# Moving a raw-word load, a key split and one ranking step within a hand-ordered slot schedule

## The chip, the cores and the metric

The kernel runs on one core of one Trainium2 chip. TensorE (PE), VectorE (DVE), ScalarE (ACT) and GpSimd (POOL) each work through a queue of their own; SyncE (SP) issues all transfers between device memory and on-chip memory. The metric is the device time of one launch in microseconds (us), lower is better.

## What is computed

Three stages follow each other: clustered attention (a query sees only keys of its own cluster), a rational-function layer with two matrices, and a soft mixture of experts. The change lies in the first stage, which also turns the 64-bit weights of the second into 32-bit words on the side.

```python
def _attn_ref(q, k, v, centroids):          # q, k, v: (2, 8, 768, 64), centroids: (8, 16, 64)
    q_assign = np.argmax(np.einsum('bhsd,hcd->bhsc', q_n, c_n), axis=-1)
    k_assign = np.argmax(np.einsum('bhsd,hcd->bhsc', k_n, c_n), axis=-1)
    mask = q_assign[:, :, :, None] == k_assign[:, :, None, :]
    scores = np.where(mask, scale * np.matmul(q, k.transpose(0, 1, 3, 2)), -1e9)
    attn = softmax(scores)
    return np.matmul(attn, v)

def _moe_ref(x, w_in, w_out, a, b):         # w_in (512, 2048), w_out (2048, 512): float64 in memory
    h = x @ w_in
    g = (a[0] + a[1]*h + a[2]*h**2 + a[3]*h**3) / (1 + |b[0]|*|h| + |b[1]|*h**2 + 1e-6)
    return g @ w_out                        # then _moe2_ref: soft routing to 8 experts
```

## The kernel before

**Attention.** Two heads make a pair, and there are 8 pairs (0 to 7). The loop over `n` runs in slots, 12 for a pair, 96 in all; a slot treats one block of 128 queries of one head. In slot `n` PE transposes the exponentials of block `n` (`turn`, line 401, tile sT), multiplies queries by keys for block `n + 2` (`a1_mm`, lines 377 and 378, tile s) and adds to the product with v (`a2_av`, line 414). DVE takes the row maximum of s and copies it out (`a1_neg`, line 386, tile e), ACT takes the exponential (`a1_exp`, line 390) and copies the transposes to eT (`turned`, line 407). There is one bank pair for s and one for sT: PE may not begin the scores of block `n + 3` before DVE has read those of `n + 2`, nor the transposes of `n + 1` before ACT has copied those of `n`.

**Preparing a pair.** `prep(P)` prepares pair P while pair P - 1 (and the end of P - 2) is in the slots. It returns a table of rows (offset, engine, step), added at slot 12(P - 2) + 4. The steps are the ranking of clusters (`scores`, `scT`, `best`, and the three DVE steps `first(0..2)`, lines 268, 270 and 273, that make the one-hot rows), its transpose on PE (`ohT`, line 278), the copy and count on ACT (`count`, line 286, two halves), the mask weights on DVE (`masks`, lines 292 to 295, tile W), which wait for the count, and matmuls with W (`nonhot`, line 300; `alive`, line 313). `ksplit` splits the raw keys on POOL into a rounded part ka (line 239) and a rest kb (line 242), and SP sends them in six transfers (line 246) into the key operands, which pair P - 2 uses until its last scores. Pair 0 and pair 1 have orders of their own; pair 2 has the offsets of the early steps one higher (`b`).

**Decoding.** 32 blocks of raw 64-bit weight words, even ones of w_in and odd ones of w_out, go through `decode_steps`. Decode i has slot 2 + 53i // 20: three slots before it SP loads the raw words (`dma`, line 522, class "S"), in its slot DVE takes them apart (`bits`, lines 528 and 529), then `mant` (DVE, line 535) and `expo` (ACT, line 532) one slot later, `sign` (DVE, line 539) two, `value` (POOL, line 544) three, `parts` (POOL, lines 553 and 554) four. There are two raw buffers: the load for decode i waits until `sign` of decode i - 2 has read the buffer.

**What sets the order.** PE, ACT, DVE and POOL run in the order in which the loop writes the steps: in each slot first `run(n, (...))` with the classes D0, D, D1, D2 (DVE), G0, G (POOL) and S (raw loads), then the slot's main work with the classes A, P and T between. SP's order is set by the scheduler of the framework from the place in the program and its own estimate of when things are ready. A step of class G also issues the transfers that follow it (`ksplit`, `qsplit`, `parts`).

Of the kernel before, what the change touches and what calls it, by code (L numbers as in the profile page):

```python
# [58 lines left out]
def tile_kernel(ctx, tc, qT, kT, v, cenT, cenP, consts, constsb, ab, w_in, w_out, phi, w1, w2, out, dbg=None):  # L59
# [3 lines left out]
    B, NPB, _, S = qT.shape  # L63
    H = 2 * NPB
    D = v.shape[4]
# [70 lines left out]
    def load(p, names="kq"):  # L136
        b, hp = divmod(p, H // 2)
        r = raws.setdefault(p, {})
        for n in names:
            r[n] = raw_p.tile([128, S], F32, tag="raw" + n, name="raw" + n, bufs=2)  # L140
            SP.dma_start(r[n], (kT if n == "k" else qT)[b, hp])

    def load_v(p):
        b, hp = divmod(p, H // 2)
        vs[p] = v_p.tile([128, 2, 6, D], F32, tag="v", name="vt")
        SP.dma_start(vs[p], v[p])
# [68 lines left out]
    def prep(p):  # L215
# [6 lines left out]
        def tile_(pool, tag, shape, dt):  # L222
            hold[tag] = pool.tile(shape, dt, tag=tag, name=tag)
            return hold[tag]
# [28 lines left out]
        def best(c):  # L253
            if c == 0:
                tile_(s2_p, "mx", [128, 6, 4], F32)
                tile_(t_p, "eq", [128, 6, 4, 16], BF16)
            mv = hold.pop(("m", c))[:, 0:HS].rearrange("p (i g c) -> p i g c", i=3, g=4)[:, :, :, 0:16]
            mc = hold["mx"][:, 3 * c:3 * c + 3, :]
            DVE.tensor_reduce(mc, mv, AX.X, ALU.max)
            DVE.tensor_tensor(hold["eq"][:, 3 * c:3 * c + 3], mv,  # L260
                              mc.unsqueeze(3).to_broadcast([128, 3, 4, 16]), ALU.is_equal)

        def first(i):
            rank = cb[:, B_RANK:B_END].unsqueeze(1).to_broadcast([128, 24, 16])
            e3 = hold["eq"].rearrange("p i g c -> p (i g) c")
            m3 = hold["mr"] if i else tile_(s2_p, "mr", [128, 24], BF16)
            if i == 0:
                DVE.tensor_tensor(e3, e3, rank, ALU.mult)
            elif i == 1:
                DVE.tensor_reduce(m3, e3, AX.X, ALU.max)  # L270
            else:
                hold["oh"] = hold["eq"]
                DVE.tensor_tensor(e3, e3, m3.unsqueeze(2).to_broadcast([128, 24, 16]), ALU.is_equal)
# [60 lines left out]

        if p == 0:
            return first_pair(r, o, locals())
        b = 1 if p == 2 else 0
        return [
            (1 + b, "T", lambda: scores(0)),
            (2 + b, "A", lambda: scaled(0)),  # L340
# [3 lines left out]
            (4 + b, "D0", lambda: best(0)),  # L344
            (4 + b, "P", lambda: scT(1)),
            (5 + b, "D0", lambda: best(1)),
            (6, "D0", lambda: first(0)),
            (6, "G", ksplit),
            (7, "D0", lambda: first(1)),
            (8, "D0", lambda: first(2)),  # L350
            (8, "P", ohT),
            (9, "A", count),
            (10, "D0", masks),
            (10, "P", lambda: nonhot(0)),
            (11, "A", lambda: signed(0)),
# [12 lines left out]
    def a1_mm(u):  # L368
        p, idx = divmod(u, 12)
        half, rest = divmod(idx, 6)  # L370
        i, h = divmod(rest, 2)
        o = ops[p % NBUF][h]
        it = slice((3 * half + i) * 128, (3 * half + i + 1) * 128)
        ps = s1s[u] = psS[u == 1].tile([128, 2, 512], F32, tag="S", name="s1")
        for c in range(2):
            w = slice(c * HS, (c + 1) * HS)
            PE.matmul(ps[:, c, 0:HS], o["q1"][:, it], o["k1"][:, w], start=True, stop=False)  # L377
            PE.matmul(ps[:, c, 0:HS], o["q2"][0:80, it], o["k2"][0:80, w], start=False, stop=True)  # L378
# [9 lines left out]
    def a1_exp(u):  # L388
        g, rest = divmod(u, 6)
        ACT.activation(es[u], es[u], AF.Exp, scale=-1.0, bias=nvs[g][:, rest:rest + 1], accum_out=sums[g][:, rest:rest + 1])  # L390
# [3 lines left out]
    def turn(u):  # L394
        g, rest = divmod(u, 6)
        if rest == 0:
            eTs[g] = e_p.tile([128, 2, 6, HS], F32, tag="eT", name="eT", bufs=2)
        e = es.pop(u).rearrange("p c (j t) -> p (c j) t", j=3)
        ps = eTp[u] = psS[1].tile([128, 2, 512], F32, tag="S", name="sT")
        for j in range(6):  # L400
            PE.transpose(ps[:, j // 3, j % 3 * 128:(j % 3 + 1) * 128], e[:, j, :], ident)  # L401

    def turned(u):
        g, rest = divmod(u, 6)
        i, h = divmod(rest, 2)
        dst = eTs[g][:, h, :, i * 128:(i + 1) * 128].rearrange("p (c j) t -> p c j t", c=2)
        ACT.copy(dst, eTp.pop(u)[:, :, 0:HS].rearrange("p c (j t) -> p c j t", j=3))  # L407
# [37 lines left out]
    def a2_x(g):  # L445

        p, half = divmod(g, 2)
        b, c = divmod(p, H // 2)
        t0 = b * S + half * HS
        hold = {}  # L450

        def scale():
            hold["x"] = s2_p.tile([128, HS], F32, tag="x", name="x", bufs=1)
            DVE.tensor_tensor(hold["x"], av.pop(g)[:, 0:HS], Rs.pop(g), ALU.mult)

        def split():
            done = 0
            while done < HS:
                t, off = divmod(t0 + done, TB)
                n = min(HS - done, TB - off)  # L460
                src = hold["x"][:, done:done + n]
                dh, dl = xh[t][:, c, off:off + n], xl[t][:, c, off:off + n]
                POOL.tensor_scalar(dh, src, 1.0, 1.0, ALU.mult, ALU.mult)
                POOL.tensor_tensor(dl, src, dh.bitcast(F32), ALU.subtract)
                done += n

        return [(0, "D0", scale), (1, "G", split)]
# [11 lines left out]
    def idle(n):  # L479
        for _ in range(n):  # L480
            PE.matmul(rest_ps, zero[:, 0:128], zero, start=True, stop=True)
# [130 lines left out]
    def open_w():  # L612
        pctx.close()
        keep = ctx.enter_context(tc.tile_pool(name="keep", bufs=1, reuse_waits="tile"))
        return keep, bctx.enter_context(tc.tile_pool(name="wsp", bufs=2 * WAHEAD + 1, reuse_waits="tile"))

    def w_load(n):
        for a in range(2):
            wsp[n, a] = w_p.tile([128, NCC, 128], F32R, tag="w", name="w")
            SP.dma_start(wsp[n, a].rearrange("p c n -> p (c n)").bitcast(F32),  # L620
                         w_in2[n % NF][:, a].rearrange("p c n -> p (c n)"))
# [5 lines left out]
    def add(slot, steps):  # L627
        for off, eng, fn in steps:
            plan.setdefault(slot + off, {}).setdefault(eng, []).append(fn)

    def run(slot, engines):
        for eng in engines:
            for fn in plan.get(slot, {}).pop(eng, []):
                fn()
# [22 lines left out]
    for n in range(-LEAD, NSL + 6):  # L657
        p, k = divmod(n, 12)
        if n == -LEAD:
            load_v(0)  # L660
            load(2, "k")
        if n == 1:
            load(2, "q")
        if n == 2:
            load_v(1)
        if k == 4 and n > 0 and p + 2 < NP:
            add(n, prep(p + 2))
        if k == 6 and 0 < p < NP - 1:
            load_v(p + 1)
        if n > 0 and k == 0 and p + 2 < NP and p:  # L670
            load(p + 2, "q")
        if n > 0 and k == 1 and p + 2 < NP and p:
            load(p + 2, "k")
        if n == NSL - OPENW:
            keep, w_p = open_w()
            for i in range(WAHEAD):
                w_load(i)
        g, rest = divmod(n - 6, 6)
        if 0 < g < 2 * NP and rest == 0:
            add(n, a2_x(g - 1))  # L680
        if n == NSL + 4:
            add(n, a2_x(g))
        if n == NSL - 8:
            DVE.tensor_scalar(ncoef, coef, -1.0, None, ALU.mult)
            DVE.tensor_tensor(babs, coef[:, 4:6], ncoef[:, 4:6], ALU.max)
        run(n, ("D0", "D", "D1", "D2", "G0", "G", "S"))
        if 0 <= n < NSL:
            turn(n)
        if pend is not None:
            a1_exp(pend)  # L690
            pend = None
        if 0 <= n < NSL:
            turned(n)
        run(n, "A")
        if n + LEAD < NSL:
            pend = n + LEAD
            if n > 0 or n == -LEAD:
                a1_mm(pend)
            a1_neg(pend)
            if n < 0:  # L700

                a1_mm(n + 1 + LEAD)
        run(n, "P")
        if n >= NSL:
            if n < NSL + 2:
                a2_av(g, range(3 * rest, 3 * rest + 3))
        elif g >= 0:
            a2_av(g, (rest,))
        run(n, "T")
        if n < 6:  # L710
            idle(2 if n < -1 else 3)
# [448 lines left out]
```

## Time and profile before

| | us |
|---|---|
| median of three runs | 553.69 (551.89 to 554.3) |
| the profiled execution, its own time | 553.21 |
| span of its instructions | 551.2 |
| PE busy / DVE / ACT / POOL | 525.4 / 415.1 / 380.9 / 274.7 |

The span is the time from the first to the last instruction; 2.0 us of the execution lie outside it. The attention slots end near 298 us, the other two stages follow. A row of the timeline has its start, its length, the engine, the line, the operation and the tiles (written <- read), and in square brackets the idle time of the engine ahead of it and what ended that. PEld rows, the weight loads, are left aside: they overlap PE.

### The profile page before, as it was taken

What the parts mean: (1) busy time and instruction counts of PE and PEld (TensorE: products, weight loads), DVE (VectorE), ACT (ScalarE), POOL (GpSimd) and SP (SyncE); (2) the same over time, 40 slices, a digit from 0 to 9 for tenths busy, and PEclk for the clock granted to TensorE, in tenths of its full rate; (3) what the DMA queues carried; (4) which work ended last, traced back from release to release, by engine and by line L of the source; (5) the groups of instructions that cost most, each with busy time, mean ns of one, the idle gap of its engine ahead of it and who ended that gap; (6) DMA issues with size and microseconds to landing.
All of it is one profiled execution on the core that took longest, in us unless ns stands there. A gap on an engine that the chain in (4) does not pass through costs nothing.

```text
span 551.2 us, 10063 instructions
## 1 busy us (share of the span) xinstructions
PE 525.4 (95%) x3518; PEld 342.8 (62%) x3521; DVE 415.1 (75%) x801; ACT 380.9 (69%) x693; POOL 274.7 (50%) x314
## 2 busy tenths in 40 slices
PE   8989999899998999999999999999999999988994
PEld 3555566556565665665666777777777767643463
DVE  5688889789797788888742699999799988941143
ACT  2787887778878788797874688878587868820111
POOL 3436476567565576756623655565455535501000
PEclk9999999999999999999999999999999999998999
DMA  8949869588595885946431576766567656479996
GB/s 244 285 131 246 232 201 263 183 222 257 200 246 183 247 226 177 260 168 173 142 114 49 175 256 228 289 229 227 186 223 279 230 181 224 185 307 389 419 414 231
DMA packets 43282, 125.71 MB, mean 228 GB/s; under 512 B 6432, under 2 KB 7328, under 8 KB 38624
## 3 DMA queue, kind: packets, MB, share of 16 engines
q1 hardware_dynamic: 43232, 125.07, 69.7%
q8 instruction: 28, 0.46, 0.3%
q14 instruction: 22, 0.18, 0.1%
HBM read 89.66 MB, written 15.73 MB: 191 GB/s over the span
## 4 chain that ended last, share of the span: by engine, by line
PE 68%; DVE 11%; DMA 9%; ACT 6%; issue 2%; POOL 2%; SPq 1%; DVEq 0%; ACTq 0%; POOLq 0%
PE h L777 9%; PE h L780 8%; PE h L778 8%; PE av L414 7%; PE sT L401 7%; DMA raw<-w_out 4%; PE s L377 4%; PE gt L838 3%; PE s L378 3%; DVE e L386 3%; DMA raw<-w_in 3%; PE pb L1012 3%; PE pb L1083 3%; PE l L844 2%; PE dg L902 2%
## 5 line engine op out<-in xcount | busy, mean ns | idle before, releaser
L390 ACT ACTIVATE e<-e,nv 128x768 f32<-128x768 f32 x96 | 89.9, 936 | 45.2 <-DVE e L386 33.2
L386 DVE TENSOR_SCALAR_CACHE_REDUCE e<-s 128x768 f32<-128x768 f32 x96 | 91.5, 953 | 37.3 <-PE s L378 30.5
L401 PEld LDWEIGHTS sT<-cst,e 128*128 128x128 f32 x576 | 61.4, 140 | 51.3 <-ACT eT L407 19.1
L401 PE MATMUL sT<-cst,e 128*128 128x128 f32 x576 | 83.8, 282 | 0.7 <-ACT eT L407 0.6
L407 ACT COPY eT<-sT 128x768 f32<-128x768 f32 x96 | 75.7, 788 | 10.1 <-PE sT L401 9.2
L414 PE MATMUL av<-eT,vt 128*64 128x384 f32 x384 | 82.1, 510 | 0.0
L777 PE MATMUL h<-xh,w 128*128 128x512 f32 x192 | 80.6, 420 | 0.0
L377 PE MATMUL s<-k,q 128*128 128x384 f32 x192 | 73.3, 382 | 7.4 <-DVE pres L292 3.7
L544 POOL TENSOR_TENSOR w<-mh,ex 128x516 f32<-128x516 f32 x32 | 41.6, 1299 | 70.0 <-DVE ex L539 33.4
L778 PE MATMUL h<-xl,w 128*128 128x512 f32 x192 | 75.9, 395 | 0.0
L808 POOL TENSOR_SCALAR q<-u,babs 128x512 f32<-128x512 f32 x47 | 36.2, 770 | 73.9 <-ACT u L806 73.9
L378 PE MATMUL s<-k,q 80*128 80x384 f32 x192 | 64.8, 338 | 0.0
L810 POOL TENSOR_TENSOR q<-q,u 128x512 f32<-128x512 f32 x47 | 61.0, 1297 | 3.8
L780 PE MATMUL h<-xh,w 128*128 128x512 f32 x192 | 52.8, 396 | 0.0
L806 ACT ACTIVATE u<-h 128x512 f32<-128x512 f32 x47 | 27.9, 594 | 28.3 <-PE h L780 25.4
L777 PEld LDWEIGHTS h<-xh,w 128*128 128x128 f32 x192 | 36.2, 189 | 16.0 <-DVE r L826 3.4
L809 DVE TENSOR_TENSOR p<-p,h 128x512 f32<-128x512 f32 x47 | 32.1, 683 | 14.8 <-ACT p L807 14.6
L377 PEld LDWEIGHTS s<-k,q 128*128 128x128 f32 x192 | 36.4, 190 | 10.8 <-DVE e L386 4.8
L780 PEld LDWEIGHTS h<-xh,w 128*128 128x128 f32 x192 | 36.3, 189 | 8.9
L778 PEld LDWEIGHTS h<-xl,w 128*128 128x128 f32 x192 | 36.2, 189 | 7.2 <-issue 0.5
L817 ACT ACTIVATE r<-q,epsc 128x512 f32<-128x512 f32 (+1 forms) x49 | 33.8, 690 | 8.1 <-POOL q L810 6.7
L825 DVE SCALAR_TENSOR_TENSOR p<-p,ncoef,r 128x512 f32<-128x512 f32 (+1 forms) x49 | 35.8, 731 | 2.4 <-ACT r L818 1.8
(179 smaller groups left out, 1003.0 us busy)
## 6 DMA issues: line engine op xcount, KB each, us to landing
wt<-w SPq DMA_DIRECT2D x32, 1024.0 KB, 7.6
w<-w_in SPq DMA_DIRECT2D x96, 256.0 KB, 3.1
raw<-w_in SPq DMA_DIRECT2D x16, 512.0 KB, 5.0
raw<-w_out SPq DMA_DIRECT2D x16, 512.0 KB, 5.4
w_in<-w SPq DMA_DIRECT2D x16, 512.0 KB, 4.0
k<-ka SPq DMA_DIRECT2D x32, 192.0 KB, 5.9
q<-qh SPq DMA_DIRECT2D x28, 192.0 KB, 5.2
w_out<-w SPq DMA_DIRECT2D x16, 256.0 KB, 4.6
```

The costliest lines, as they stand in the source:

```text
L377: PE.matmul(ps[:, c, 0:HS], o["q1"][:, it], o["k1"][:, w], start=True, stop=False)
L378: PE.matmul(ps[:, c, 0:HS], o["q2"][0:80, it], o["k2"][0:80, w], start=False, stop=True)
L386: DVE.tensor_scalar(e, s1s.pop(u)[:, :, 0:HS], -1.0, None, ALU.mult, ALU.min, accum_out=nvs[g][:, rest:rest + 1])
L390: ACT.activation(es[u], es[u], AF.Exp, scale=-1.0, bias=nvs[g][:, rest:rest + 1], accum_out=sums[g][:, rest:rest + 1])
L401: PE.transpose(ps[:, j // 3, j % 3 * 128:(j % 3 + 1) * 128], e[:, j, :], ident)
L407: ACT.copy(dst, eTp.pop(u)[:, :, 0:HS].rearrange("p c (j t) -> p c j t", j=3))
L414: PE.matmul(av[g][64 * h:64 * h + 64, 0:HS], vs[g // 2][:, h, j, :], eTs[g][:, h, j, :], start=(j == 0), stop=(j == 5))
L544: POOL.tensor_tensor(w.rearrange("p (r n) -> p r n", r=3), hold["mh"].bitcast(F32), hold["ex"].bitcast(F32), ALU.mult)
L777: PE.matmul(h, wh[:, c, :], xh[t][:, c, :], start=(c == 0), stop=False)
L778: PE.matmul(h, wh[:, c, :], xl[t][:, c, :], start=False, stop=False)
L780: PE.matmul(h, wl[:, c, :], xh[t][:, c, :], start=False, stop=(c == NCC - 1))
L810: POOL.tensor_tensor(q, q, u, ALU.mult)
```

## The change

Three edits. The raw load of a slot (class S) is written ahead of the slot's POOL steps (class G), so ahead of the transfers which those steps issue. `ksplit` moves from offset 6 to 8: slot 12(P - 2) + 12 where it was 12(P - 2) + 10, for pairs 2 to 7. For pairs 3 to 7 the steps `first(0)`, `first(1)`, `first(2)`, `ohT` and `count` move one slot forward (earlier); `masks` and all after it stay. Pairs 0 and 1 keep their order; nothing is added or removed.

```diff
-        b = 1 if p == 2 else 0
+        b, c = (1, 0) if p == 2 else (0, -1)
...
-            (6, "D0", lambda: first(0)),
-            (6, "G", ksplit),
+            (6 + c, "D0", lambda: first(0)),
+            (8, "G", ksplit),
...
-            (9, "A", count),
+            (9 + c, "A", count),
...
-        run(n, ("D0", "D", "D1", "D2", "G0", "G", "S"))
+        run(n, ("D0", "D", "D1", "D2", "G0", "S", "G"))
```

SP's queue where pair 3's keys are sent (slots 20 to 25): raw_148 is the buffer of even decodes, raw_149 that of odd ones, `w_in<-w` sends a decoded block away, `k<-ka` and `k<-kb` are the key operands. Before:

```order
L522 DMA raw_148<-w_in 128x1024
L555 DMA w_in_146<-w_1111 128x1024
L246 DMA k_1_0_127<-ka 64x768 x2
L246 DMA k_1_1_131<-ka 64x768 x2
L246 DMA k_1_0_128<-kb 64x768
L246 DMA k_1_1_132<-kb 64x768
L522 DMA raw_149<-w_out 128x1024
L548 DMA w_out_147<-w 128x512
```

The same place after the change:

```order
L522 DMA raw_148<-w_in 128x1024
L555 DMA w_in_146<-w_1113 128x1024
L522 DMA raw_149<-w_out 128x1024
L548 DMA w_out_147<-w 128x512
L246 DMA k_1_0_127<-ka 64x768 x2
L246 DMA k_1_1_131<-ka 64x768 x2
L246 DMA k_1_0_128<-kb 64x768
L246 DMA k_1_1_132<-kb 64x768
```

The load of decode 9 (raw_149) and the sending of decode 7 stand ahead of the six key transfers instead of behind them.

SP's queue at pair 5 (slots 44 to 50), where the loads are those of decodes 17, 18 and 19. Before:

```order
L522 DMA raw_149<-w_out 128x1024
L548 DMA w_out_147<-w 128x512
L246 DMA k_1_0_127<-ka 64x768 x2
L246 DMA k_1_1_131<-ka 64x768 x2
L246 DMA k_1_0_128<-kb 64x768
L246 DMA k_1_1_132<-kb 64x768
L522 DMA raw_148<-w_in 128x1024
L141 DMA rawk<-kT 128x768
L555 DMA w_in_146<-w_2089 128x1024
L522 DMA raw_149<-w_out 128x1024
```

After:

```order
L522 DMA raw_149<-w_out 128x1024
L548 DMA w_out_147<-w 128x512
L522 DMA raw_148<-w_in 128x1024
L555 DMA w_in_146<-w_2082 128x1024
L246 DMA k_1_0_127<-ka 64x768 x2
L246 DMA k_1_1_131<-ka 64x768 x2
L246 DMA k_1_0_128<-kb 64x768
L246 DMA k_1_1_132<-kb 64x768
L522 DMA raw_149<-w_out 128x1024
L141 DMA rawk<-kT 128x768
```

The load of decode 18 comes ahead of the keys; that of decode 19 (the second raw_149) now stands right behind them.

ACT's queue around pair 3's count (slots 24 and 25): e is the exponential, eT the copy of transposes, wT a copy for the decoding, oT with cnt the count. Before:

```order
L390 ACTIVATE e,ssum<-e,nv 128x768
L407 COPY eT<-sT 128x6x128
L573 COPY wT<-mf 128x512
L286 ACTIVATE oT,cnt<-mb 64x3x128 x2
L390 ACTIVATE e,ssum<-e,nv 128x768
```

The same five rows after the change:

```order
L286 ACTIVATE oT,cnt<-mb 64x3x128 x2
L390 ACTIVATE e,ssum<-e,nv 128x768
L407 COPY eT<-sT 128x6x128
L573 COPY wT<-mf 128x512
L390 ACTIVATE e,ssum<-e,nv 128x768
```

The count moved ahead of one exponential and one copy of the main work; the other engines' queues move in the same way.

## Rows read from the trace of the kernel before

**Rows 1.** Window: length, then busy us of PE, PEld, DVE, ACT, POOL; clock; DMA:

```profile
57.15:298.00 240.85, 232.08 (x1566) 148.14 (x1565) 190.92 (x395) 192.17 (x353) 142.37 (x168) 1.00 0.68 198
```

**Rows 2.** Timeline: PE's waits at the preparation of pairs 3 to 7:

```profile
100.01 0.45 PE L377 MATMUL s<-k,q 128*128 128x384 f32 x1 [2.22 <-DVE pres L292]
...
123.82 0.44 PE L377 MATMUL s<-k,q 128*128 128x384 f32 x1 [0.25 <-DVE e L386]
...
135.71 0.34 PE L300 MATMUL mf<-oT,W 80*128 80x384 bf16 x1 [0.35 <-DVE W L295]
...
171.02 0.45 PE L377 MATMUL s<-k,q 128*128 128x384 f32 x1 [1.49 <-DVE pres L292]
...
206.79 0.34 PE L300 MATMUL mf<-oT,W 80*128 80x384 bf16 x1 [0.46 <-DVE W L295]
...
209.46 0.44 PE L377 MATMUL s<-k,q 128*128 128x384 f32 x1 [0.73 <-DVE e L386]
...
242.17 0.34 PE L300 MATMUL mf<-oT,W 80*128 80x384 bf16 x1 [0.37 <-DVE W L295]
```

**Rows 3.** Timeline: DVE's two long waits for raw words (decodes 9 and 18):

```profile
97.79 0.69 DVE L528 TENSOR_SCALAR ex<-raw 128x516 int32<-128x516 int32 x1 [2.00 <-DMA raw<-w_out]
...
168.81 0.69 DVE L528 TENSOR_SCALAR ex<-raw 128x516 int32<-128x516 int32 x1 [1.34 <-DMA raw<-w_in]
```

**Rows 4.** Timeline: DVE's waits for the count, pairs 4, 6 and 7:

```profile
135.00 0.20 DVE L293 TENSOR_SCALAR pres<-cnt 32x1 f32<-32x1 f32 x1 [1.30 <-ACT oT L286]
...
206.08 0.20 DVE L293 TENSOR_SCALAR pres<-cnt 32x1 f32<-32x1 f32 x1 [1.49 <-ACT oT L286]
...
241.20 0.20 DVE L293 TENSOR_SCALAR pres<-cnt 32x1 f32<-32x1 f32 x1 [0.70 <-ACT oT L286]
```

**Rows 5.** Timeline: SP issuing keys and raw loads, pairs 3 and 5:

```profile
88.20 1.31 SPq L246 DMA_DIRECT2D k<-kb  x2
90.05 0.33 SPq L522 DMA_DIRECT2D raw<-w_out  x1
...
161.34 0.48 SPq L522 DMA_DIRECT2D raw<-w_in  x1
```

**Rows 6.** Timeline: DVE's sign steps that free the buffers of decodes 9 and 18:

```profile
86.84 1.30 DVE L539 SCALAR_TENSOR_TENSOR ex<-raw,ex 128x516 int32<-128x516 int32 x1
...
158.46 0.68 DVE L539 SCALAR_TENSOR_TENSOR ex<-raw,ex 128x516 int32<-128x516 int32 x1
```

**Rows 7.** Transfers: KB and us to landing of the loads issued at 199.58 and 207.36:

```profile
raw<-w_out SPq DMA_DIRECT2D x1, 512.0 KB, 5.7
...
raw<-w_in SPq DMA_DIRECT2D x1, 512.0 KB, 3.1
```

**Rows 8.** Timeline and group of line 286: ACT and PE around pair 3's count:

```profile
95.69 0.78 ACT L407 COPY eT<-sT 128x768 f32<-128x768 f32 x1
...
96.92 0.88 PE L401 MATMUL sT<-cst,e 128*128 128x128 f32 x6
...
L286 ACT ACTIVATE oT<-mb 64x384 bf16<-64x384 bf16 x16 | 7.7, 482 | 3.7 <-PE mb L278 3.6
```

**Rows 9.** Timeline of POOL and DVE around pair 5's split:

```profile
154.92 0.83 POOL L239 TENSOR_SCALAR ka<-rawk 128x768 fp32r<-128x768 f32 x1
155.83 2.42 POOL L242 TENSOR_TENSOR kb<-rawk,ka 128x384 fp32r<-128x384 f32 x2
...
155.99 1.40 DVE L535 SCALAR_TENSOR_TENSOR mh<-raw,mh 128x516 f32<-128x516 uint32 x1
...
164.85 1.60 POOL L554 TENSOR_TENSOR w<-w,w 128x512 fp32r<-128x512 f32 x1
...
175.46 0.69 DVE L528 TENSOR_SCALAR ex<-raw 128x516 int32<-128x516 int32 x1
...
177.50 0.96 DVE L386 TENSOR_SCALAR_CACHE_REDUCE e<-s 128x768 f32<-128x768 f32 x1 [0.75 <-PE s L378]
```

**Rows 10.** Group of line 268: the step first(0):

```profile
L268 DVE TENSOR_TENSOR eq<-eq,cb 128x384 bf16<-128x384 bf16 x8 | 3.4, 427 | 0.1
```

More of the change, by code (lines that the diff above doesn't have):

```diff
@@ L346, in prep @@
             (5 + b, "D0", lambda: best(1)),
-            (6, "D0", lambda: first(0)),
-            (6, "G", ksplit),
-            (7, "D0", lambda: first(1)),
-            (8, "D0", lambda: first(2)),
-            (8, "P", ohT),
-            (9, "A", count),
+            (6 + c, "D0", lambda: first(0)),
+            (8, "G", ksplit),
+            (7 + c, "D0", lambda: first(1)),
+            (8 + c, "D0", lambda: first(2)),
+            (8 + c, "P", ohT),
+            (9 + c, "A", count),
             (10, "D0", masks),
```

## The prediction

> **What bounds the kernel now.** I read first the busy time of the engines over the attention slots: in 240.9 us from slot 12 on PE is busy 232.1, DVE 190.9, ACT 192.2, POOL 142.4, at a granted clock of 1.00 [rows 1]. PE bounds this stage, and an edit that takes nothing out of PE's work can win no more than the 8.8 us for which PE stands idle there. The change lies in this stage alone; the two later stages run after it and would shift as a whole.
>
> Second, where PE waits in the slots that the change touches, those around the preparation of pairs 3 to 7 [rows 2]. The reader is to see two long waits, 2.22 us (pair 3) and 1.49 us (pair 5), at a scores matmul, and short ones: 0.35, 0.46 and 0.37 us at the first matmul with the mask weights W (pairs 4, 6, 7), and 0.73 us at a scores matmul right after pair 6's. The 0.25 us at 123.82 is another kind, DVE late with a row maximum.
>
> Third, what DVE waits for just before each. The label of the two long ones, `pres`, is the next row on DVE and no cause. Ahead of it DVE had stood 2.00 and 1.34 us for raw words [rows 3], and everything behind, the row maximum that frees the scores bank included, was late by that much. Ahead of the short ones DVE stood 1.30, 1.49 and 0.70 us for ACT's count [rows 4]. So two causes: two raw loads that land late, and a count that ends late.
>
> Fourth, why the loads are late. The load for decode 9 was issued at 90.05, right behind the last key transfers at 88.20 [rows 5], while `sign`, which frees its buffer, ended at 86.84 + 1.30 = 88.14 [rows 6]. It landed 97.79 - 90.05 = 7.7 us later. For decode 18 `sign` ended at 158.46 + 0.68 = 159.14 [rows 6], the issue came at 161.34 [rows 5], the landing 7.5 us later at 168.81 [rows 3]. A load with nothing ahead of it lands in 3.1 us [rows 7]. So 1.9 and 2.2 us were lost in SP's queue, and some 4 us more behind the bytes of six key transfers.
>
> **The change, part by part.**
>
> *Loads ahead of the keys.* At pair 3 the load of decode 9, at pair 5 that of decode 18 now stands ahead of the six key transfers, and the keys are split two slots later. It can go at 88.1 and 159.1 and has 97.79 - 2.00 - 88.1 = 7.7 us and 168.81 - 1.34 - 159.1 = 8.4 us until DVE asks. Even 5.7 us, the landing of a load issued behind keys but with little else ahead [rows 7], fits. I take both DVE waits as gone. For PE that is 2.22 + 1.49 = 3.7 us, unless something else is late next.
>
> *What is late next there: ACT.* The count now stands ahead of an exponential and a copy eT of the main work. It is two halves of 0.48 us, 1.0 us together [rows 8]. At pair 3 the copy ended at 95.69 + 0.78 = 96.5 and PE began the next transposes, which need its bank, at 96.92. Delayed by 1.0 the copy ends near 97.5: PE waits 0.6 us where it did not. I charge 0.6 at pair 3 and, as an estimate by the same row, 0.6 at pair 5; zero if ACT runs earlier because DVE does. At pairs 4, 6 and 7 I charge nothing: DVE, for whose row maxima ACT's exponentials wait, stands idle 0.70 to 1.49 us there [rows 4] and will run earlier by that. Without this cover it would be 0.6 each.
>
> *The count one slot forward.* A slot is 240.9 / 84 = 2.9 us [rows 1], so the count ends 1.0 to 2.9 us earlier, against DVE waits of 0.70 to 1.49. All three should go, and with them PE's 0.35 + 0.46 + 0.37 and, since DVE is then on time, the 0.73 behind pair 6's: 1.9 us in all.
>
> *The ranking one slot forward.* DVE's work is the same, but the slot that has `best(1)` now also has `first(0)`, 0.43 us [rows 10], ahead of its row maximum. At pair 4 that row maximum is the one for which PE already waits 0.25 at 123.82, so this wait should grow by 0.4. At pairs 3, 5, 6 and 7 PE shows no wait there; I charge 0.4 for one of the four, and keep 0 and 1.6 as the bounds.
>
> *The key split two slots later.* Its operands are used from ten slots later on, some 29 us: nobody waits for the keys themselves. What waits is what is queued behind: on POOL the steps xh, rb and `value`, which come 0.8 + 2.4 = 3.3 us later [rows 9] and are asked for more than a slot afterwards; on SP the loads behind the keys. At pair 5 that is decode 19. POOL ends `parts` at 164.85 + 1.60 = 166.4, then ka and kb at 169.7, two kb transfers of 0.65 each follow [rows 5], and the load goes near 171.0. With 3.1 us it lands at 174.1, with 5.7 at 176.7; DVE asks for it at 175.46 - 1.34 = 174.1 [rows 9]. So DVE waits 0 to 2.6 us, of which 0.75, its present wait for PE at 177.50, is covered [rows 9]: 0 to 1.9 us on PE. I take 0, since the slots behind it hold extra PE work, and keep 1.9 for the range and for a rival.
>
> [...] At 155.99 the DVE step of line 535 took 1.40 us beside POOL's kb; the sign step of the same shape took 0.68 alone at 158.46 [rows 6, 9]. Kb will now meet another DVE step, so I count 0.7 lost for 0.7 won. [...]
>
> **The sum.** Won: 3.7 + 1.9 = 5.6. Given back: 0.6 + 0.6 on ACT, 0.4 + 0.4 on DVE, 2.0. Net 3.6 us. The span goes from 551.2 to 547.6, the execution, with 2.0 us around the span, from 553.2 to 549.6. The profiled execution is 0.5 below the median of 553.69, so the median goes to **550.1 us**. With nothing given back it is 548.1; with four times 0.4 on DVE and 0.6 at four pairs on ACT (1.6 + 2.4 = 4.0, net 1.6) 552.1.
>
> **The rivals.**
>
> 1. *The wait moves from decode 18 to decode 19.* For it: SP's new order at pair 5, and a POOL that is 3.3 us later. Against it: DVE has slack two slots on. Price 1.9 us: 550.1 + 1.9 = 552.0.
> 2. *Kb meets the wrong DVE steps.* In the slots right behind the split DVE makes W and the row maxima for which PE waits; if at each of the six pairs the 0.7 us falls on PE's path, while in the place before it lay beside PE work, the price is 6 x 0.7 = 4.2: 554.3, no change. Against it: the split met such a step before as well [rows 9], so the place changes and not the number.
> 3. *The loads land as late as before.* If the landing is set by the bytes already under way (the query transfers ahead) and not by SP's order, only the count's 1.9 is won and the 2.0 lost: 553.8. Against it: the key bytes were among those ahead.
> 4. *Slower: loads caught behind later keys.* The keys now go in the slots in which the next loads are due (decodes 10, 15 and 19 at pairs 3, 4 and 5). A load that needs the 7.7 us seen at decode 9 instead of 3.1 loses 4.6 us; if its time before DVE asks is shorter than that by 2.5 at three pairs, 7.5 us are lost against 3.6 won: 557.6. It decides where POOL ends kb later than the `sign` that frees the next buffer. At pair 5 it does by the working above; elsewhere I find it only by a little or not at all.
>
> **How the numbers follow.** Forecast 0.52 (548.1 to 552.1); rival 1 0.15; rival 2 0.12; rival 3 0.12; rival 4 0.09. A measurement of this kernel can tell 0.5%, 2.8 us, from no change: faster is below 550.9, slower above 556.5. Of the forecast's own range some 0.42 of its 0.52 lies below 550.9, of the rivals 0.04: 0.46 faster. Slower is most of rival 4: 0.08. The rest, 0.46, is the same. The range is 547.5 to 554.5: below it I leave 0.03, above it rival 4 and the upper tail of rivals 2 and 3, 0.15.
>
> **What would show it.** In the profile after: DVE's idle ahead of line 528 without a 2 us entry, decode 9's load issued near 88, decode 18's near 159 on the old clock; PE's waits at `pres` gone; DVE's wait at line 293 gone for pairs 3 to 7 and still there for pairs 1 and 2. New waits of PE at sT for a copy eT, 0.6 each, would show ACT's price; a DVE wait for raw words near slot 52 rival 1; line 535 and 539 with a higher mean rival 2. I am wrong if PE's idle time in the attention stage does not fall by 2 to 6 us, or if it falls and the later stages give it back.

## The result and the profile after

The changed kernel took 547.78 us (median of four runs, 546.47 to 549.21) against 553.85 for the kernel before on the same chip: a ratio of 0.9897, 95% interval 0.9852 to 0.9943, faster by 1.0% or 6.1 us. Repeated later it gave 548.11 us and 0.9895 (0.9860 to 0.9929). The prediction said 550.1 us, 547.5 to 554.5.

The profiled execution took 547.26 us, its span 545.5. The window table of both kernels, from the first PE transposes of slot 12 to those of slot 95 (length, then busy us of PE, PEld, DVE, ACT, POOL; granted clock; DMA), first before, then after:

```profile
57.15:294.93 237.78, 229.01 (x1550) 146.06 (x1548) 190.26 (x393) 190.99 (x351) 142.29 (x167) 1.00 0.69 201
```

```profile
56.72:290.71 233.99, 228.77 (x1551) 145.85 (x1549) 189.86 (x393) 190.89 (x351) 144.92 (x170) 1.00 0.69 204
```

PE's busy time differs by 0.2 us; the time in which it stands idle fell from 8.8 to 5.2 us, so these slots are 3.8 us shorter. Of the 5.95 us between the two profiled executions, 3.79 lie here, 0.43 ahead of slot 12 (near 52 us PE waits 0.82 us for query operands before and 0.33 after), 1.48 behind slot 95, 0.25 outside the span.

PE's waits that answer to [rows 2], timeline after:

```profile
64.23 0.34 PE L300 MATMUL mf<-oT,W 80*128 80x384 bf16 x1 [0.45 <-DVE W L295]
...
96.18 0.87 PE L401 MATMUL sT<-cst,e 128*128 128x128 f32 x6 [0.26 <-ACT eT L407]
98.36 0.34 PE L300 MATMUL mf<-oT,W 80*128 80x384 bf16 x1 [0.61 <-DVE W L295]
121.75 0.44 PE L377 MATMUL s<-k,q 128*128 128x384 f32 x1 [0.66 <-DVE e L386]
...
191.26 0.44 PE L377 MATMUL s<-k,q 128*128 128x384 f32 x1 [0.22 <-DVE e L386]
204.71 0.44 PE L377 MATMUL s<-k,q 128*128 128x384 f32 x1 [0.17 <-DVE e L386]
228.64 0.45 PE L377 MATMUL s<-k,q 128*128 128x384 f32 x1 [0.20 <-DVE e L386]
231.89 0.44 PE L377 MATMUL s<-k,q 128*128 128x384 f32 x1 [0.35 <-DVE e L386]
```

The 2.22 and 1.49 us at `pres` are gone, so are the waits for W at pairs 4, 6 and 7 and the 0.73 behind pair 6's; pair 2's W wait (64.23) was there before. From pair 3 on the waits sum to 2.47 us, against 5.87 in [rows 2]. Waits of PE that both kernels have are left out, as in [rows 2] (line 313 near 140 and 175, line 377 near 252).

SP and DVE where the loads of decodes 9, 18 and 19 are issued, answering to [rows 5, 6], the transfers issued at 86.97 and 156.57 (KB, us to landing), and the two kinds of DVE wait that are left, answering to [rows 3, 4]:

```profile
86.25 0.69 DVE L539 SCALAR_TENSOR_TENSOR ex<-raw,ex 128x516 int32<-128x516 int32 x1
86.97 0.33 SPq L522 DMA_DIRECT2D raw<-w_out  x1
...
155.85 0.70 DVE L539 SCALAR_TENSOR_TENSOR ex<-raw,ex 128x516 int32<-128x516 int32 x1
156.57 0.33 SPq L522 DMA_DIRECT2D raw<-w_in  x1
...
165.91 1.33 SPq L246 DMA_DIRECT2D k<-kb  x2
167.33 0.54 SPq L522 DMA_DIRECT2D raw<-w_out  x1
```

```profile
raw<-w_out SPq DMA_DIRECT2D x1, 512.0 KB, 4.2
...
raw<-w_in SPq DMA_DIRECT2D x1, 512.0 KB, 3.4
```

```profile
63.53 0.20 DVE L293 TENSOR_SCALAR pres<-cnt 32x1 f32<-32x1 f32 x1 [1.49 <-ACT oT L286]
...
173.74 0.69 DVE L528 TENSOR_SCALAR ex<-raw 128x516 int32<-128x516 int32 x1 [1.91 <-DMA raw<-w_out]
```

Both loads now go within 0.03 us of the `sign` that frees their buffers, land 4.2 and 3.4 us later (7.7 and 7.4 before), and DVE does not wait for them. The count wait is left at pairs 0, 1 and 2 alone. One raw wait is new: decode 19's load stands behind the moved keys and lands 6.3 us after its issue, so DVE stands 1.91 us. PE shows no wait for it.

### The profile page after: what moved, and what is told of

The parts are those of the page before. It is cut to its first block, busy times and chain, and to the rows that moved or that the text cites. A ratio compares the mean times of both kernels' runs of the same rounds, so it can differ in the third digit from the quotient of the medians.

```text
span 545.5 us, 10069 instructions
## 1 busy us (share of the span) xinstructions
PE 524.1 (96%) x3518; PEld 342.3 (63%) x3521; DVE 414.0 (76%) x801; ACT 381.0 (70%) x693; POOL 274.5 (50%) x314
## 4 chain that ended last, share of the span: by engine, by line
PE 75%; DVE 11%; ACT 5%; DMA 4%; issue 3%; SPq 1%; POOL 1%; DVEq 0%; POOLq 0%; ACTq 0%
PE av L414 10%; PE sT L401 9%; PE h L777 9%; PE h L780 8%; PE h L778 8%; PE s L377 5%; PE s L378 4%; DVE e L386 4%; PE gt L838 4%; PE pb L1083 3%; PE pb L1012 3%; PE l L844 2%; PE dg L902 2%; PE mf L230 1%; ACT e L390 1%
```

## The experiments

Slots are cut at the start of PE's transposes (line 401) in the one execution that was profiled of each kernel; slots 20 to 95 are called the stage below. The changed kernel has two such profiles, and their slots 20 to 95 differ by 1.0 us (210.35 and 211.32), so a difference of that size in this column is not shown by it alone. The ratio is to runs of the kernel before on the same chip; "all its runs" are the 88 made beside the experiments, on four chips. The last column counts runs whose mean granted clock was 0.994 or less.

| kernel | time, us | ratio to before (95%) | slots 20 to 95, us | low-clock runs |
|---|---|---|---|---|
| before (all its runs) | 553.82 | | 213.8 | 52 of 88 |
| loads first alone | 551.59 | 0.9962 (0.9931 to 0.9993) | 213.1 | 1 of 10 |
| keys later alone | 552.90 | 0.9968 (0.9942 to 0.9994) | 215.4 | 0 of 10 |
| ranking earlier alone | 550.91 | 0.9970 (0.9934 to 1.0005) | 213.1 | 4 of 10 |
| loads and keys | 553.74 | 1.0004 (0.9976 to 1.0031) | 214.8 | 2 of 10 |
| keys and ranking | 548.55 | 0.9893 (0.9843 to 0.9943) | 210.4 | 1 of 4 |
| all three, again | 548.11 | 0.9895 (0.9860 to 0.9929) | 211.3 | 0 of 6 |
| before, waits filled | 551.87 | 0.9987 (0.9957 to 1.0018) | 213.0 | 1 of 12 |
| pair 5's keys later still | 549.20 | 0.9925 (0.9896 to 0.9955) | 212.0 | 2 of 10 |
| ranking in shared slots | 548.29 | 0.9909 (0.9873 to 0.9945) | 210.4 | 2 of 6 |
| the same, last pair as before | 545.44 | 0.9856 (0.9817 to 0.9894) | 209.6 | 0 of 5 |
| after, long waits put back | 556.88 | 1.0059 (1.0030 to 1.0089) | 219.0 | 12 of 12 |
| after, long waits elsewhere | 556.38 | 1.0055 (1.0027 to 1.0083) | 218.9 | 8 of 12 |

**Loads first, alone.**

```diff
-        run(n, ("D0", "D", "D1", "D2", "G0", "G", "S"))
+        run(n, ("D0", "D", "D1", "D2", "G0", "S", "G"))
```

> Only the raw load is written ahead of the slot's POOL steps; the key split and the ranking stay. In SP's queue this moves decode 9's load ahead of two of the six key transfers at pair 3, decode 18's ahead of one at pair 5. Theory K (the waits for raw words come from the key transfers ahead, so the split's two slots take them away, and this edit does little): DVE's wait at decode 9 falls from 2.00 to about 0.5 and at decode 18 from 1.34 to about 0.7, PE's last transposes start 1 to 2 us before 294.9. Theory L (the place of the load in the slot takes them away): both waits 0, last transposes near 291.5, 3.5 us earlier. The count's waits stay at 1.3 to 1.5 in both.

PE's two waits at `pres` and DVE's raw wait for decode 9, timeline:

```profile
95.33 0.69 DVE L528 TENSOR_SCALAR ex<-raw 128x516 int32<-128x516 int32 x1 [0.81 <-DMA raw<-w_out]
97.55 0.45 PE L377 MATMUL s<-k,q 128*128 128x384 f32 x1 [0.75 <-DVE pres L292]
...
169.86 0.44 PE L377 MATMUL s<-k,q 128*128 128x384 f32 x1 [0.99 <-DVE pres L292]
```

The edit shortens the waits and does not remove them: SP now sends load 9 ahead of two of the six key transfers, no more, and load 18 ahead of one, and they land 7.8 and 8.1 us after their issue, as late as before. Slots 20 to 32 are 1.4 us shorter, but slots 32 to 44 are 1.0 longer. There `first(2)` (line 273), 0.56 us in the kernel before, began while POOL's `value` (line 544) was under way:

```profile
126.16 1.29 POOL L544 TENSOR_TENSOR w<-mh,ex 128x516 f32<-128x516 f32 x1 [1.52 <-DMA w_out<-w]
126.32 1.55 DVE L273 TENSOR_TENSOR eq<-eq,mr 128x384 bf16<-128x384 bf16 x1
```

In the kernel before `value` began at 128.42, 0.03 us behind `first(2)` at 128.39, and it was `value` that took longer (1.69 us for 1.29). In all the stage is 0.8 us shorter.

**Keys later, alone.**

```diff
-            (6, "G", ksplit),
+            (8, "G", ksplit),
```

> Only the key split moves two slots later. Theory K: both waits for raw words are gone (0.2 at most), a new one of some 1.9 us comes for decode 19, the count's waits stay and new ones appear at pairs 3 and 5, where DVE is now early; PE's last transposes start 2.5 to 3.5 us before 294.9. Theory L: the waits stay at 2.0 and 1.3, last transposes within 0.5 of 294.9.

The raw waits of decodes 9 and 18 are gone, so it is this edit that clears SP's queue; yet slots 20 to 95 became 1.6 us longer, where a gain was expected. The median of its runs is 0.8 us below the kernel before all the same, since none of them had a low clock; its runs at 0.997 or more have a median of 552.7 us, against 551.4 for those of the kernel before on that chip, so they are 1.3 us longer too. The cause stands on DVE, shown here at pairs 4 and 5, in the rows around `first(2)` with POOL's `value` and `parts` (lines 544 and 554), and DVE's count wait and PE's wait for W behind it:

```profile
126.35 1.29 POOL L544 TENSOR_TENSOR w<-mh,ex 128x516 f32<-128x516 f32 x1 [2.84 <-PE mf L569]
126.69 1.37 DVE L273 TENSOR_TENSOR eq<-eq,mr 128x384 bf16<-128x384 bf16 x1
...
134.12 0.20 DVE L293 TENSOR_SCALAR pres<-cnt 32x1 f32<-32x1 f32 x1 [1.49 <-ACT oT L286]
135.02 0.34 PE L300 MATMUL mf<-oT,W 80*128 80x384 bf16 x1 [0.74 <-ACT e L390]
...
162.54 1.28 POOL L554 TENSOR_TENSOR w<-w,w 128x512 fp32r<-128x512 f32 x1
162.59 1.65 DVE L273 TENSOR_TENSOR eq<-eq,mr 128x384 bf16<-128x384 bf16 x1
```

With the split gone from its old place, POOL's two-input steps run just when DVE comes to `first(2)`, which takes 1.37 and 1.65 us there; at pair 6 it meets `value` (1.06 us), at pair 7 the second half of the split itself (1.40 us). It ends 0.42 us after POOL's step in both places shown (128.06 against 127.64, 164.24 against 163.82). The transpose of the one-hot rows and the count are later by that. At pair 3 it is W itself (line 295) that meets `parts`: 1.41 us, 0.46 in the kernel before. PE pays at W: 0.86, 0.74 (its row names ACT's e), 0.37, 0.46 and 0.66 us at pairs 3 to 7, where [rows 2] has 0, 0.35, 0, 0.46 and 0.37, and besides 0.35 to 0.40 at three row maxima that had no wait. One new wait cost more than its bracket: slot 37 grew by 0.64 us for 0.35; the scores matmul had begun 0.24 us before the end of the transposes ahead of it. The transfers gained what this edit promised; DVE lost more.

**Ranking earlier, alone.**

```diff
-        b = 1 if p == 2 else 0
+        b, c = (1, 0) if p == 2 else (0, -1)
...
-            (6, "D0", lambda: first(0)),
+            (6 + c, "D0", lambda: first(0)),
```

`first(1)`, `first(2)`, `ohT` and `count` get the same `+ c`.

> Only the ranking steps and the count come one slot earlier for pairs 3 to 7. Additive theory: the count's waits of DVE (1.30, 1.49, 0.70) are gone, both waits for raw words stay near 2.0 and 1.3, and PE's last transposes start 0.7 to 1.5 us before 294.9 (1.9 won, 0.4 to 1.2 given back on DVE and ACT). Rival (the two causes hide each other): no gain, because the raw waits grow by what the count no longer costs: within 0.3 of 294.9.

All count waits of pairs 3 to 7 are gone. Of the raw waits, decode 9's stays:

```profile
97.57 0.69 DVE L528 TENSOR_SCALAR ex<-raw 128x516 int32<-128x516 int32 x1 [1.82 <-DMA raw<-w_out]
...
97.88 0.87 PE L401 MATMUL sT<-cst,e 128*128 128x128 f32 x6 [0.72 <-ACT eT L407]
99.78 0.44 PE L377 MATMUL s<-k,q 128*128 128x384 f32 x1 [1.04 <-DVE pres L292]
```

The stage is 0.8 us shorter, the same as with the first edit. Here too `first(2)` meets `value`, at pairs 3 and 5 (0.98 and 1.12 us).

**Loads and keys, without the ranking**, to see whether the parts add.

```diff
-            (6, "G", ksplit),
+            (8, "G", ksplit),
...
-        run(n, ("D0", "D", "D1", "D2", "G0", "G", "S"))
+        run(n, ("D0", "D", "D1", "D2", "G0", "S", "G"))
```

> The first two edits (raw load ahead, key split later) without the ranking edit. Theory M (the edits need each other: once the raw words are in time, DVE stands for the count instead, and the keys' POOL steps slow DVE in the slots that first(2) still fills): no raw wait of 0.5 us or more in pairs 3 to 5, count waits of 1.2 to 1.5 at pairs 4, 6 and 7, and the stretch from slot 20 to slot 95 takes 214.5 to 216, as with the key split alone (215.4), against 210.4 in the whole change. Additive theory: 211 to 212.

No gain in time, 1.0 us more in the stage, with count waits of 1.48, 1.48 and 1.24 us at pairs 4, 6 and 7: nearly the second edit's picture, with `first(2)` at 1.05 to 1.39 us at pairs 4 to 7.

**Keys and ranking, without the loads** (against the changed kernel).

```diff
-        run(n, ("D0", "D", "D1", "D2", "G0", "S", "G"))
+        run(n, ("D0", "D", "D1", "D2", "G0", "G", "S"))
```

> The change without its first edit: key split later and ranking earlier, the raw load written behind the POOL steps as before. Theory K: the same as the whole change, last transposes within 0.3 of 290.7, ratio to the kernel before near 0.99. Theory L: the waits for raw words are back, 294 or so.

This is the whole change: the stage's 210.4 us are those of the changed kernel, the time differs by less than the interval. With the keys out of the way, SP's order differs from that of the changed kernel in one row only. So the second and third edits make the gain together (−3.4 us in the stage, against +1.6 and −0.8 alone). The runs at a clock of 0.997 or more on that chip, few as they are, say the same: medians of 551.4 us before, 552.7 with the second edit, 550.1 with the third, 548.4 with both. The reason that the rows show is that the third takes `first(2)` away from the POOL steps that the second brings to it: over pairs 3 to 7 `first(2)` takes 2.8 us in the kernel before, 4.2 with the first edit alone, 6.0 with the second, 3.8 with the third and 3.4 with the second and third together. The first adds nothing that can be measured.

**Pair 5's keys two slots later still** (on the changed kernel), to remove the new wait of 1.91 us.

```diff
-            (8, "G", ksplit),
+            (10 if p == 5 else 8, "G", ksplit),
```

> The whole change, with the key split of pair 5 alone another two slots later, so that decode 19's load stands ahead of its transfers. If DVE's wait of 1.91 us for decode 19 is covered by its slack to PE: that wait is gone and the stretch from slot 44 to slot 56 stays at 34.6 (within 0.2). Rival (it cost PE time): the stretch falls by 0.5 to 1.9 us.

Decode 19's wait is gone, and slots 44 to 56 rose from 34.64 to 35.38 us, with two PE waits that the changed kernel lacks:

```profile
168.09 0.44 PE L377 MATMUL s<-k,q 128*128 128x384 f32 x1 [0.44 <-DVE pres L292]
169.51 0.34 PE L300 MATMUL mf<-oT,W 80*128 80x384 bf16 x1 [0.44 <-DVE W L295]
```

The 1.91 us had cost PE nothing, and the split at its later place, in the slot that makes W, costs 0.7: W takes 1.05 us there, 0.68 in the changed kernel.

**Ranking in shared slots, then with the last pair as before.** On the changed kernel, `first(0)` and `first(1)` share offset 6, `first(2)` and `ohT` go to 7, `count` to 8, for all pairs from 2 on:

```diff
-            (7 + c, "D0", lambda: first(1)),
-            (8 + c, "D0", lambda: first(2)),
+            (6, "D0", lambda: first(1)),
+            (7, "D0", lambda: first(2)),
```

> The whole change, with first(0) kept in its old slot together with first(1), and for pair 2 as well; ohT and count one slot earlier also for pair 2. If first(0) in the slot of best(1) is what made PE wait 0.66 at 121.75, 0.22 at 191.26 and 0.20 and 0.35 near 230 in the changed kernel, these fall to 0.25 and 0 (0.8 us won), and pair 2's wait of 0.45 for W is gone: the stretch from slot 12 to slot 95 falls from 234.0 to about 232.8. Rival (the two steps together are late in the next slot): waits of the same sum one slot later, 234.0.

Pair 4's wait of 0.66 us fell to 0.25 and pair 6's two went, pair 2's W wait of 0.45 went and slots 12 to 20 fell by 1.0, but slots 20 to 95 are no shorter, and the last pair lost: PE waited 0.60 us where the changed kernel had 0.20 (228.64 in the rows after). In time the two can't be told apart. In the next kernel pair 7 alone keeps the order of before, its split included (`first(1)`, `first(2)`, `ohT` and `count` with `+ g`):

```diff
-        b, c = (1, 0) if p == 2 else (0, -1)
+        b, g = 1 if p == 2 else 0, 1 if p == 7 else 0
...
-            (8, "G", ksplit),
+            (8 - 2 * g, "G", ksplit),
+            (6 + g, "D0", lambda: first(1)),
```

> The changed kernel with two alterations: for pairs 2 to 6 the ranking steps first(0) and first(1) share the slot at offset 6, first(2) and ohT follow at 7, the count at 8, the keys at 8 (as in the experiment before with all pairs); pair 7 keeps the order of the kernel before in full (6, 7, 8, 8, 9, keys at 6). Theory A (what a pair gains or loses is its own; pair 7 lost 0.5 us by the change and 0.4 more by the shared slot, since its count wait of 0.70 had cost PE only 0.37): slots 68 to 80 fall from 34.4 to 33.9 us, slots 12 to 95 to 232.2 us (changed kernel 234.0), and the time to about 546.5, 1 us below the changed kernel. Theory B (pair 7's gain is taken back in the slots behind, since the order of pair 6's end and pair 7's start interlock): slots 12 to 95 stay at 233 and the time at 547.8.

Slots 68 to 80 took 33.62 us (34.42 after, 33.88 before), slots 12 to 95 232.22 us as expected, and the time was 545.44 us, against 548.11 for the changed kernel on the same chip. DVE still waits for the count there, and PE does not wait for DVE at W:

```profile
234.67 0.20 DVE L293 TENSOR_SCALAR pres<-cnt 32x1 f32<-32x1 f32 x1 [0.70 <-ACT oT L286]
```

This is the fastest version of the study. For pair 7 the second and third edits together cost more than the wait that they removed: in the changed kernel `first(2)` meets the split there, and ends 0.41 us after POOL's rounding step (timeline after); here it takes 0.55 us.

```profile
228.31 0.83 POOL L239 TENSOR_SCALAR ka<-rawk 128x768 fp32r<-128x768 f32 x1
228.50 1.05 DVE L273 TENSOR_TENSOR eq<-eq,mr 128x384 bf16<-128x384 bf16 x1
```

**The rest of the gain: the granted clock.** The attention slots explain 3.8 us; the medians differ by 6. One experiment put idle matmuls into PE's two long waits of the kernel before:

```diff
+            if n in (26, 50):
+                m = m_tile()
+                for _ in range(5 if n == 26 else 3):
+                    PE.matmul(m, identb, cb[:, 0:512], start=True, stop=True)
```

> The kernel before with idle matmuls (5 in slot 26, 3 in slot 50, some 0.43 us each) ahead of the scores matmuls at which PE stands 2.22 and 1.49 us; they compute nothing that is used. PE's order and DVE's waits stay. Theory G (part of the measured gain is PE's granted clock, which falls for some microseconds in an execution after such long waits): mean clock of the runs rises from 0.994 to 0.997 and the time falls by 2 to 3 us, to 551. Rival: the drops have nothing to do with those two waits (the profiled execution of before has its drop in the last stage): clock 0.993 to 0.995 as before, time within 0.3% of the kernel before.

PE's waits there fell to 0.55 and 0.80 us. The clock was 0.9962 on average against 0.9941 in 29 runs of the kernel before on that chip, and 1 of 12 runs was at 0.994 or less against 16 of 29. The median fell by 2.1 us, but the interval of the ratio includes 1, so the clock speaks for these two waits and the time leaves it open. The changed kernel was run again:

> The changed kernel itself, run again in more rounds, for the part of its gain that the attention slots do not show. Theory A (the changed kernel has fewer falls of the granted clock than the kernel before): mean granted clock of its runs 0.997 to 0.998 against 0.994, median 547.5 to 548.0, ratio 0.988 to 0.990. Theory B (its first runs met fewer falls by chance; the falls come alike in both): mean clock about 0.995, median 548.5 to 549.5, ratio 0.991 to 0.993, that is 3.9 to 4.9 us, the attention slots' part with the opening. In both slots 20 to 95 take 210.4 +- 0.3 us in the profile.

The ten runs of the changed kernel (four of the result, six here) have a mean of 0.9966, one of them 0.994 or less; the kernel before has 0.9940 and 52 of 88. In the profile of these runs decode 8's load is late, and its slots 20 to 32 are 1 us longer than in the first profile (DVE's wait there was 0.60 in the kernel before, none in the first profile after):

```profile
89.89 0.69 DVE L528 TENSOR_SCALAR ex<-raw 128x516 int32<-128x516 int32 x1 [1.18 <-DMA raw<-w_in]
...
97.34 0.87 PE L401 MATMUL sT<-cst,e 128*128 128x128 f32 x6 [0.72 <-ACT eT L407]
```

Then the long waits were put back into the changed kernel, by work on DVE at the old places, and in a second kernel one pair later each:

```diff
-            a1_neg(pend)
+            for _ in range({25: 4, 49: 4}.get(n, 1)):
+                a1_neg(pend)
```

The second kernel has slots 37 and 61 in place of 25 and 49.

> The changed kernel in which the row maxima of slots 25 and 49 are each taken four times instead of once (same result): DVE is late by 2.9 us (3 x 0.96) at the two places at which the kernel before waited for raw words, and PE gets two waits of about 2 to 2.9 us there. Both theories: slots 20 to 95 take 4 to 5.8 us longer than the changed kernel's 210.4. Theory A (the long PE waits are what lowers the granted clock of many runs of the kernel before): 6 in 10 runs have a mean clock of 0.994 or less, as the kernel before (39 of 65), mean clock 0.994, and the median is 548.0 + 5 + 2 = 555. Theory B (the clock does not depend on these waits): 1 or 2 in 10 runs at 0.994 or less, mean clock 0.9966, median 548.0 + 5 = 553.

> The same with the row maxima of slots 37 and 61 taken four times, one pair later each, where the kernel before has no wait. Slots 20 to 95 again 4 to 5.8 us above the changed kernel's 210.4. Theory A in its general form (any PE wait of 2 us or more in the attention slots does it): mean clock 0.994, 6 in 10 runs at 0.994 or less, median 555. Theory A in its narrow form (only waits at the two old places do it) and theory B: mean clock 0.9966, median 553.

All 12 runs of the first had a clock of 0.994 or less, 0.988 on average; of the second 8 of 12, 0.992 on average. PE's two waits, timeline, and the stretch behind the first of them, window table (columns as above), first kernel:

```profile
100.15 0.42 PE L377 MATMUL s<-k,q 128*128 128x384 f32 x1 [2.22 <-DVE pres L292]
...
174.28 0.41 PE L377 MATMUL s<-k,q 128*128 128x384 f32 x1 [3.12 <-DVE pres L292]
```

```profile
97.00:100.00 3.00, 0.88 (x6) 0.64 (x6) 2.90 (x7) 0.49 (x1) 1.53 (x2) 1.00 0.74 289
100.00:101.00 1.00, 0.85 (x5) 0.71 (x5) 0.83 (x3) 0.91 (x2) 0.00 (x0) 1.00 0.71 291
101.00:102.00 1.00, 1.00 (x6) 0.33 (x5) 1.00 (x2) 1.00 (x4) 0.00 (x0) 0.56 0.07 16
102.00:103.00 1.00, 1.00 (x12) 0.20 (x8) 0.26 (x2) 1.00 (x2) 0.00 (x0) 0.50 0.00 0
103.00:104.00 1.00, 1.00 (x12) 0.71 (x5) 0.57 (x2) 0.38 (x2) 0.00 (x0) 0.50 0.00 0
104.00:105.00 1.00, 1.00 (x7) 1.00 (x7) 0.32 (x1) 0.21 (x1) 0.54 (x1) 0.73 0.00 0
105.00:110.00 5.00, 5.00 (x34) 3.21 (x33) 4.35 (x9) 3.89 (x7) 1.02 (x3) 1.00 0.44 157
```

Behind a PE wait of 2.22 us, as long as that of the kernel before, the clock fell to 0.50 at 101 us and came back between 104 and 105. The four matmuls with v took 1.55 us in the fall, at 101.23, and 0.87 us behind it, at 105.99. By an estimate from the table's clocks, 0.44 + 0.50 + 0.50 + 0.27, the fall costs PE 1.7 us. The second wait is followed by such a fall too (0.83 over 170 to 180), and in the other kernel both waits of 2.11 us are, one of them by a fall of 6.7 us, to 141 us (0.62 over 134 to 135, 0.50 to 140, 0.89 over 140 to 145). In the first kernel the waits' 5.3 us and two falls make 8.7, the 8.7 us by which slots 20 to 95 grew. So theory A holds, in its general form: it is the long wait, wherever it stands.

Two profiles show it where nobody had put a wait. Loads and keys, and keys and ranking, have a wait of 3.59 and 3.11 us for query operands ahead of slot 12 (the first of them, timeline):

```profile
35.33 0.42 PE L377 MATMUL s<-k,q 128*128 128x384 f32 x1 [3.59 <-DMA q<-ql]
```

The clock is 0.76 in the 7 us from 35 and from 34 us on. Over all kernels whose profile has no PE wait of 1.3 us or more from slot 12 on (the table's second to eleventh row and the changed kernel's first four runs), 14 of 87 runs were at 0.994 or less, against 52 of 88 of the kernel before and 20 of 24 with waits put back.

## Why the prediction was right, and where it was short

**The loads** (won 3.7). Right, and by the mechanism named: SP's queue behind the keys. Both PE waits are gone and both loads were issued where the working put them. But the gain was given in part to the wrong edit: the key split's move clears the queue, and writing the load first does nothing beyond it; alone it left the landings at 7.8 and 8.1 us.

**The count** (won 1.9). Right: 0.35, 0.46, 0.37 and 0.73 are all gone.

**ACT** (given back 0.6 and 0.6). PE waits 0.26 us for eT at pair 3 in one execution and 0.72 in the other, and not at all at pair 5. Unforeseen is the wait for W at pair 3, 0.61 and 0.26, in the same two executions; together 0.9 and 1.0 at pair 3. It comes from POOL: W, 0.46 us at 100.32 in the kernel before, meets `parts` (timeline after):

```profile
96.80 1.29 POOL L554 TENSOR_TENSOR w<-w,w 128x512 fp32r<-128x512 f32 x1
96.83 1.47 DVE L295 SCALAR_TENSOR_TENSOR W<-cb,pres 64x192 bf16<-64x192 bf16 x1
```

**DVE** (given back 0.4 at pair 4 and 0.4 at one of the others). Pair 4's wait rose from 0.25 to 0.66, by 0.4. The others show 0.22, 0.17, 0.20 and 0.35, 0.9 in all, within the bounds of 0 and 1.6.

**The sum.** Won 5.6, given back 2.2 (2.47 less the 0.25 that was there before): 3.4 against 3.6 forecast. That the sum agrees so well is in part luck: at pair 5 nothing was given back where 0.6 was charged, at pair 3 0.9 for 0.6, on DVE 1.3 for 0.8. Pair 2, left out of the working, gave 0.3 more in this execution (slots 12 to 20, 23.64 us against 23.96), but not in the repeat (23.92).

**The first rival** (the wait moves to decode 19). It did, with 1.91 us, within the 0 to 2.6 worked out. It cost PE nothing, as taken.

**The split beside DVE's steps** (0.7 lost for 0.7 won). This step failed, in both directions. In the changed kernel the meetings are fewer: the groups of lines 535 and 539 from 57 to 298 us, first before, then after:

```profile
L535 DVE SCALAR_TENSOR_TENSOR mh<-raw,mh 128x516 f32<-128x516 uint32 x28 | 25.4, 908 | 0.0
L539 DVE SCALAR_TENSOR_TENSOR ex<-raw,ex 128x516 int32<-128x516 int32 x28 | 21.1, 753 | 0.5 <-ACT ex L532 0.3
```

```profile
L535 DVE SCALAR_TENSOR_TENSOR mh<-raw,mh 128x516 f32<-128x516 uint32 x28 | 22.7, 810 | 0.0
L539 DVE SCALAR_TENSOR_TENSOR ex<-raw,ex 128x516 int32<-128x516 int32 x28 | 20.7, 738 | 0.1
```

DVE won 3.1 us in these two steps and lost 1.5 at W (line 295, 2.8 us in all before, 4.3 after), of which the row at pair 3 lay on PE's path. With the keys moved and the ranking not, it lost 0.5 to 1.1 us at `first(2)` in each of pairs 4 to 7, on PE's path. The second rival named such a price (4.2 us) and looked at the wrong partner: at pairs 4 to 6 it is not the split itself but the POOL steps that come forward when the split leaves, at pair 7 it is the split. The sum took no notice of this, since the third edit takes most of it away. What the rows show of such a meeting is that line 273 ends 0.41 or 0.42 us after POOL's step in all of them, however early it began. The 0.7 us from which I worked is near the rest of one half of the split: line 535 began 0.16 us behind it [rows 9], and a half takes about 1.97 / 2 = 0.98 us, which leaves 0.8, an estimate from the row of both halves, timeline after:

```profile
89.85 1.97 POOL L242 TENSOR_TENSOR kb<-rawk,ka 128x384 fp32r<-128x384 f32 x2
```

**The third and fourth rivals.** The loads of decodes 9 and 18 landed 3.5 and 4.0 us sooner than before, so the third is out. Loads behind the keys' new place were caught as the fourth says: decodes 10 and 15 took 6.2 and 6.7 us to land (4.8 and 3.5 before). DVE asked for them late enough and did not wait.

**What was short.** The forecast was 550.1, measured 547.8. For slots 12 to 95 the working is right to within 0.2 us in this profile (in the repeat's they gained 2.5 us); the term that is missing is the clock, and the median came within 0.3 us of the range's lower end. The profile of the kernel before showed 1.00 in the slots, and I took the wait of 2.22 us at its own length. In that one execution no fall followed it; but the profiles here without any fall have a mean clock of 0.998, and 52 of 88 runs of that kernel were at 0.994 or less. At a mean clock of 0.997 or more the kernel before takes 551.5 us (18 of its runs), the changed kernel 547.6 (6 of 10): 3.9 us, the attention slots' part. The medians differ by 5.7 us (553.82 and 548.11), so 1.8 us, the difference, go with the lower clock of the other runs. That long waits bring falls is shown by the two kernels that put waits back, and with the two old waits filled by idle matmuls fewer runs have a low clock (1 of 12). That the falls of the kernel before stand right behind its own waits is not seen: its one profile has 1.00 there.

The 1.48 us behind slot 95 in the two profiles are another fall, in line 1012's matmuls, before and after:

```profile
500.00:510.00 10.00, 8.74 (x68) 2.93 (x64) 1.04 (x2) 0.00 (x0) 1.80 (x1) 0.83 1.01 423
```

```profile
495.00:505.00 10.00, 8.74 (x84) 3.14 (x80) 1.04 (x2) 0.00 (x0) 1.81 (x1) 1.00 1.02 427
```

PE stood idle 0.88 (0.87 after) and 0.38 us just ahead of it, in both kernels, and the clock fell in one. Two of the other kernels' profiles, both with moved keys, show a fall near there too (ranking in shared slots, 0.83 over 500 to 510 us; loads and keys, 0.89 over 500 to 510 and 0.94 over 510 to 520). Nothing ties it to the change, which leaves that stage alone.

## What to carry to other kernels

Judge a moved step by what moves up into the place that it leaves, on its own engine and on the other of DVE and POOL (line 273 took up to 1.65 us beside a POOL step, 0.56 alone): two edits here were worth −3.4 us together and +1.6 and −0.8 apart, in one profile each. A wait is worth removing only where the bounding engine waits with it: 1.91 us on DVE cost nothing, and removing pair 7's 0.70 cost more than it gave. Taking away a wait of 2 us on TensorE can be worth more than its length, because the clock fell behind such waits in six of the seven that the profiles here show, at 1.7 to 3.4 us of PE's work each by an estimate; read the clock of many runs, not of one profile.

## What the runs showed of the hardware

- Behind six PE waits of 2.11 to 3.59 us the granted clock fell: to 0.50 where it was read in steps of 1 or 2 us (long waits put back, 2.22 us; long waits elsewhere, 2.11; keys and ranking, 3.11), to a mean of 0.83 over 170 to 180 us (long waits put back, 3.12), of 0.97 and 0.86 over 200 to 210 and 210 to 220 us (long waits elsewhere, 2.11) and of 0.76 over 7 us (loads and keys, 3.59). By an estimate from these clocks five of the falls took 1.7 us of PE's work each; one lasted 6.7 us and took 3.4. It doesn't always fall: the kernel before shows 1.00 behind 2.22 us in its profile.
- A two-input DVE step (line 273, bf16, 0.56 us alone) that began while a POOL step was under way ended 0.41 or 0.42 us after it in the rows shown: 1.37 and 1.65 us (keys later alone) and 1.55 (loads first alone) beside two-input steps, 1.05 (changed kernel) beside the one-input step of line 239. Line 295 ended 0.21 us after `parts` (1.47 us, changed kernel). Where DVE began 0.03 us sooner it was POOL's step that took longer, 1.69 us for 1.29 (kernel before).
- The 512 KB loads issued right behind six key transfers of 192 KB landed 5.4 to 7.7 us after their issue (five loads of the kernel before, 90.05 to 231.41 us) and 6.3 in the changed kernel (167.33); those of decodes 9 and 18, ahead of the keys there, landed in 4.2 and 3.4, that of [rows 7] at 207.36 in 3.1.
